# Holding back the loads of later batches, and new lengths for transfers in a planned kernel

## The chip, the cores and the metric

One core of one Trainium2 chip. The metric is the device time of one execution in microseconds (us). A kernel's figure is the median of its runs. A profiled execution has one span of its own, which is not the median. "Fast" and "slow" are the two states of a run; only fast runs enter the ratios.

## The reference

Attention whose keys and values are first projected from 1024 rows to 64, then an MLP over the tokens with a residual, then an MLP over the channels with a residual. Eight batches, eight heads, head size 64.

```python
def _attn_ref(q, k, v, E, F):
    k_proj = np.einsum('ks,bhsd->bhkd', E, k)
    v_proj = np.einsum('ks,bhsd->bhkd', F, v)
    ...  # softmax of q k_proj^T / 8
    return np.matmul(attn, v_proj)

def _moe_ref(x, w_tok1, w_tok2, w_ch1, w_ch2):
    xt = x.transpose(0, 2, 1)
    h = np.maximum(xt @ w_tok1, 0.0) @ w_tok2
    u = x + h.transpose(0, 2, 1)
    h2 = np.maximum(u @ w_ch1, 0.0) @ w_ch2
    return u + h2
```

## The kernel before

The kernel is software-pipelined over batches by a planner. Every piece of work is a job with an engine, an occupancy and a latency; the planner lays all jobs out in time by a simple model and the kernel then emits them in that order. The times of the model serve only to set the order. The kernel pins each engine's instructions to the order in which they are emitted, so on the chip an engine takes its jobs in that order and waits only for its data. The model knows one serial "DMA" engine, although loads go out from GpSimd's queue and transposes and stores from SyncE's. The page of the kernel before counts both queues against the same 16 DMA engines (q0, the loads, 43.2% of their time, and q1 29.4%), and a transpose of u beside loads lands late: 14.3 us after its issue at 137.82, behind five loads, against 4.2 at 90.0 behind one.

```python
    LAG = {"PE": 0.25, "DVE": 0.15, "ACT": 0.15, "POOL": 0.2, "DMA": 0.1}
    ...
    def sp(t, fn, **kw):                       # a transpose or a store, issued by SyncE
        return pl.add("DMA", t, t + 1.5, fn, **kw)

    def ld(mb, fn, **kw):                      # a load, issued by GpSimd
        t = mb / 0.40
        return pl.add("DMA", t, t + 2.0, fn, **kw)
    ...
    def q_transpose(due):
        for h in range(0, H, H // 2):
            sp(
                5.0,                           # planned length of a transpose of q
                lambda h=h: nc.sync.dma_start_transpose(out=qT[...], in_=q_sb[...]),
    ...
            sp(
                4.0,                           # planned length of a transpose of u
                lambda: nc.sync.dma_start_transpose(out=uT_t[i]..., in_=u_t[b % 2]...),
```

Per batch there are six loads (k, k, v, v, q, q: four heads each), two transposes of q into qT and two transposes of u into uT (each 128 x 2048 elements of 2 bytes, 512 KB). Right behind each uT come four sums and differences of quarters of uT on VectorE, the "S sums", which the channel MLP multiplies. VectorE's later work, such as the x_sb that TensorE needs for the next batch, stands behind the S sums in its order, so a late uT stops VectorE and then TensorE: in the trace before, VectorE waited 6.69 us for uT (until 152.17) and TensorE 6.46 us for x_sb (until 153.44).

The loads of batch b + 2 are made as jobs at the end of batch b's part:

```python
        if b + 2 < B:
            for name in "kvq":
                for hh in range(0, H, H // 2):
                    load_heads(b + 2, name, hh, H // 2, None)

    plan = pl.plan()
    for j in plan:
        j.fn()
        pin()
```

The softmax here doesn't subtract the row's maximum and nothing guards it: scores larger than these inputs give would overflow.

Of the kernel before, what the change touches and what calls it, by code (L numbers as in the profile page):

```python
# [12 lines left out]
ACT = mybir.ActivationFunctionType  # L13
# [21 lines left out]
class Planner:  # L35


    LAG = {"PE": 0.25, "DVE": 0.15, "ACT": 0.15, "POOL": 0.2, "DMA": 0.1}

    def __init__(self, caps, homes):  # L40
        self.jobs, self.caps, self.homes = [], caps, homes
# [30 lines left out]
    def plan(self):  # L72
# [15 lines left out]
        def open_(j):  # L88
            est[j.n] = max((d.end + self.LAG[d.eng] if d.eng != j.eng else d.full for d in j.deps), default=0.0)
            can.setdefault(j.eng, []).append(j)  # L90
# [83 lines left out]
def kernel(  # L174
# [13 lines left out]
    nc = tc.nc  # L188
# [27 lines left out]
    def pin():  # L216
        done = nc.cur_bb.bb.instructions
        for i in done[seen[0] :]:
            before = last.get(i.engine)
            if before is not None:  # L220
                tc.add_manual_dep(i, before, order, reason="program order")
            last[i.engine] = i.name
        seen[0] = len(done)
# [5 lines left out]
    def tile_of(shape, dtype, name):  # L229
        return sb.tile(shape, dtype, tag=name, name=name)  # L230
# [3 lines left out]
    def bank(b):  # L234

        return banks[b.at]
# [3 lines left out]
    o_t = [tile_of([P, 2, DM], F32, f"o{i}") for i in range(3)]  # L240
# [36 lines left out]
    for half in range(2):  # L277
# [3 lines left out]
    pl = Planner(  # L281
        {"U": 5, "D": 3, "F": 3, "S": 7},
        {"U": range(6), "D": range(6), "F": (5, 6, 7), "S": (0, 1, 2, 3, 4, 6, 7)},
    )
    MM = {512: 0.216, 256: 0.109, 130: 0.057, 128: 0.057, 64: 0.057}

    def pe(n, cols, fn, **kw):
        t = n * MM[cols]
        return pl.add("PE", t, t, fn, **kw)
# [11 lines left out]
        return pl.add("POOL", t, t, fn, **kw)  # L301

    def sp(t, fn, **kw):
        return pl.add("DMA", t, t + 1.5, fn, **kw)

    def ld(mb, fn, **kw):
        t = mb / 0.40
        return pl.add("DMA", t, t + 2.0, fn, **kw)


    def dma(dst, src):
        return lambda: nc.gpsimd.dma_start(out=dst, in_=src)

    def load_heads(b, name, h, hn, due):
        dst, src = {"k": (k_sb, k), "v": (v_sb, v), "q": (q_sb, q)}[name]
        hs = slice(h, h + hn)
        ld(
            0.262 * hn,
            dma(dst[:, hs], src[b, hs].rearrange("h (p si) d -> p h si d", p=P)),
            writes=[(name, i) for i in range(h, h + hn)], prio=due,  # L320
        )

    first = iter(range(-1000, 0))
    ld(1.0, dma(EF[0], E), writes=["E"], prio=next(first))
# [36 lines left out]
    def due_d(j, i):  # L361
        return TU * j + 23.8 + 1.76 * i
# [22 lines left out]
    for n, (src, dst) in enumerate(((EF[0], ET_sb), (EF[1], FT_sb))):  # L385
        b = Bank("F", full=False)
# [111 lines left out]
    def q_transpose(due):  # L498
        for h in range(0, H, H // 2):
            sp(  # L500
                5.0,
                lambda h=h: nc.sync.dma_start_transpose(
                    out=qT[:, h : h + H // 2].rearrange("p h j s -> p (h j) s"),
                    in_=q_sb[:, h : h + H // 2].rearrange("p h si d -> p (h si d)"),
                ),
                reads=[("q", i) for i in range(h, h + H // 2)],
                writes=[("qT", i) for i in range(h, h + H // 2)], prio=due,
            )
# [96 lines left out]
    def token2(b, si, due):  # L605
        bk = Bank(stream[0], full=False)

        def mm():
            for t in range(TC):
                nc.tensor.matmul(  # L610
                    bank(bk), wt2_sb[:, t, si::NSI], hT_sb[:, t, :],
                    start=(t == 0), stop=(t == TC - 1),
                )

        pe(
            TC, 512, mm, reads=["wt2"] + [("hT", t, hp) for t in range(TC) for hp in range(HP)],
            takes=[bk], prio=due,
        )
        dve(
            512,  # L620
            lambda: nc.vector.tensor_add(  # L621
                out=u_t[b % 2][:, si, :], in0=bank(bk), in1=x_sb[:, si, :]
            ),
            reads=[("x", h, si // NJ) for h in range(H)], writes=[("u", b % 2, si)], uses=[bk],
        )
        if si % NJ == NJ - 1:
            i = si // NJ
            sp(
                4.0,
                lambda: nc.sync.dma_start_transpose(  # L630
                    out=uT_t[i].rearrange("p s dc q -> p (s dc) q"),
                    in_=u_t[b % 2][:, i * NJ : (i + 1) * NJ].rearrange("p s d -> p (s d)"),
                ),
                reads=[("u", b % 2, n) for n in range(i * NJ, (i + 1) * NJ)],
                writes=[("uT", i, n) for n in range(HP)], prio=None,
            )
# [210 lines left out]
    out_v = out.rearrange("b (p si) d -> b p si d", p=P)  # L847

    def down_block(j):
        b, i = j // 2, j % 2  # L850
        G = G_t[j % 2]
        bk = {n: Bank("D", seeded=n == "y") for n in "xyz"}
        os = [(2 * j + sh) % 3 for sh in range(2)]

        def view(n):
            return bank(bk[n]).rearrange("p (t d) -> p t d", t=2)

        def u_of(sh, dh):
            rows = slice(i * NJ + 2 * sh, i * NJ + 2 * sh + 2)
            return u_t[b % 2][:, rows, dh * DH : (dh + 1) * DH]  # L860

        def u_key(sh):
            rows = range(i * NJ + 2 * sh, i * NJ + 2 * sh + 2)
            return [("u", b % 2, r) for r in rows] + ([("up", hp, i) for hp in range(HP)] if b == 0 else [])

        def o_of(sh, dh):
            return o_t[os[sh]][:, :, dh * DH : (dh + 1) * DH]

        def o_key(sh, dh):
            return ("o", os[sh], dh)  # L870

        def mm(n, t):
            for cc in range(C2):
                nc.tensor.matmul(  # L874
                    view(X_OF[n])[:, t, :], G[:, G_OF[n], cc, t * P : (t + 1) * P], w2_of(n, cc),
                    start=(n in (1, 7) and t == 0 and cc == 0), stop=(cc == C2 - 1),
                    skip_group_check=True,
                )

        def product(n, i):  # L880
            if n in (1, 2, 3):
                w = [("w2", {1: 0, 2: 1, 3: 1}[n], c) for c in range(2)]
            else:
                w = [("W2", c, n) for c in range(2)]
            bb = bk[X_OF[n]]
            for t in range(2):
                first = n in (1, 7) and t == 0
                pe(
                    C2, 256, lambda t=t: mm(n, t),
                    reads=w + [("G", j % 2, G_OF[n], m) for m in range(SETS)],  # L890
                    takes=[bb] if first else [], uses=[] if first else [bb],
                    prio=due_d(j, 2 * i + t),
                )

        def store(sh):
            rows = slice(i * NJ + 2 * sh, i * NJ + 2 * sh + 2)
            sp(
                2.0, lambda: nc.sync.dma_start(out=out_v[b, :, rows, :], in_=o_t[os[sh]]),
                reads=[o_key(sh, 0), o_key(sh, 1)], prio=None,
            )  # L900

        def copy_add(dst, key, src, sh, dh):
            act(512, lambda: nc.scalar.copy(out=dst, in_=view(src)), writes=[key], uses=[bk[src]])  # L903
            pool(
                512, lambda: nc.gpsimd.tensor_add(out=dst, in0=dst, in1=u_of(sh, dh)),  # L905
                reads=u_key(sh), writes=[key],
            )

        product(1, 0)
        act(  # L910
            512, lambda: nc.scalar.copy(out=view("y"), in_=view("x")), takes=[bk["y"]],
            uses=[bk["x"]],
        )
        product(7, 1)
        product(6, 2)
        copy_add(db, "db", "y", 1, 0)
        product(2, 3)
        copy_add(o_of(0, 0), o_key(0, 0), "x", 0, 0)
        product(5, 4)
        dve(  # L920
            512, lambda: nc.vector.tensor_add(out=da, in0=view("y"), in1=u_of(1, 1)),  # L921
            reads=u_key(1), writes=["da"], uses=[bk["y"]],
        )
        dve(
            512, lambda: nc.vector.tensor_add(out=o_of(1, 1), in0=view("z"), in1=da),  # L925
            reads=["da"], writes=[o_key(1, 1)], uses=[bk["z"]],
        )
        product(3, 5)
        copy_add(o_of(0, 1), o_key(0, 1), "y", 0, 1)
        store(0)  # L930
        product(4, 6)
        dve(
            512, lambda: nc.vector.tensor_add(out=o_of(1, 0), in0=view("z"), in1=db),
            reads=["db"], writes=[o_key(1, 0)], uses=[bk["z"]],
        )
        store(1)


# [51 lines left out]
    for b in range(B):  # L990
# [10 lines left out]
        if b + 2 < B:  # L1001
            for name in "kvq":
                for hh in range(0, H, H // 2):
                    load_heads(b + 2, name, hh, H // 2, None)

    plan = pl.plan()
    for j in plan:
        j.fn()
        pin()


# [28 lines left out]
```

## Time and profile before

| | before |
|---|---|
| median of 4 runs | 450.68 us (448.52 to 452.01) |
| profiled span | 452.1 us, mean TensorE clock 0.974 |

The prediction below shows the page, the windows with TensorE's four holes, and the chain. What it does not show is where the loads of batch 3 stand near the two uT transposes of batch 1, which were issued at 90.0 and 93.4 us. The timeline of GpSimd of the kernel before; columns are start and length of the issue, engine, line, operation, tiles, count, and in brackets what it waited for:

```profile
86.50 0.78 POOL L312 DMA_DIRECT2D k_sb<-in_k_dram  x1 [5.40 <-PE ps L445]
...
95.38 0.78 POOL L312 DMA_DIRECT2D k_sb<-in_k_dram  x1
96.15 1.50 POOL L312 DMA_DIRECT2D v_sb<-in_v_dram  x2
97.63 1.51 POOL L312 DMA_DIRECT2D q_sb<-in_q_dram  x2
```

One k load goes out 3.5 us ahead of the first transpose, and the other five behind the second. The view of the uT tile for 80 to 125 us gives landing times of 4.2 to 4.3 us, and nobody waits for them.

### The profile page before, as it was taken

The numbers are of one execution on the slowest core, as the hardware profiler recorded it, in microseconds if no ns is written. First come the engines' busy times: TensorE is split into PE (matmuls) and PEld (weight loads), VectorE is DVE, ScalarE is ACT, GpSimd is POOL, SyncE is SP. The second block draws the span as 40 slices with busy tenths as digits, with TensorE's granted clock in tenths as the row PEclk, the third lists the DMA queues.
The fourth block names the chain that finished last, engine by engine and source line by source line (L and its number), as shares of the span: only waits on it lengthen the run. The fifth ranks groups of instructions, "written<-read, shape, count | busy, mean of one in ns | idle before, by whom it ended". The sixth has DMA issues, their size and how long they took to land.

```text
span 452.1 us, 9325 instructions
## 1 busy us (share of the span) xinstructions
PE 420.0 (93%) x3736; PEld 338.3 (75%) x3736; DVE 324.0 (72%) x791; ACT 235.2 (52%) x431; POOL 106.5 (24%) x122
## 2 busy tenths in 40 slices
PE   4789999999999499997999999997999999999993
PEld 2578878677878378786787878786787877888883
DVE  2479989589887366977676885887677885875451
ACT  1347674367466154575447744575446654465530
POOL 7443041240041120412114021411102021213212
PEclk8599999999999799999999999999999999999998
DMA  8999989899959927899756996299150502240122
GB/s 118 207 202 205 207 131 175 167 186 206 186 82 196 197 41 160 150 168 188 141 127 105 203 160 141 51 183 228 54 94 1 141 1 95 48 139 39 57 95 93
DMA packets 89515, 60.63 MB, mean 134 GB/s; under 512 B 55680, under 2 KB 84864, under 8 KB 89472
## 3 DMA queue, kind: packets, MB, share of 16 engines
q0 software_dynamic: 30784, 29.63, 43.2%
q1 hardware_dynamic: 58688, 30.41, 29.4%
q8 instruction: 29, 0.48, 0.4%
q14 instruction: 14, 0.11, 0.1%
HBM read 59.24 MB, written 16.78 MB: 168 GB/s over the span
## 4 chain that ended last, share of the span: by engine, by line
PE 71%; DVE 13%; DMA 12%; issue 2%; ACT 1%; POOL 1%; DVEq 0%; ACTq 0%; POOLq 0%
PE ps L874 26%; PE ps L779 25%; DMA uT<-u 10%; PE ps L590 5%; PE ps L610 5%; PE ps L442 3%; DVE G L814 2%; PE ps L536 2%; PE ps L559 2%; DVE S L649 2%; DMA q_sb<-in_q_dram 2%; DVE x_sb L576 1%; DVE wT L403 1%; DVE u L706 1%; PE ps L520 1%
## 5 line engine op out<-in xcount | busy, mean ns | idle before, releaser
L874 PEld LDWEIGHTS <-G 128*128 128x128 bf16 x1344 | 130.6, 98 | 26.9 <-issue 3.8
L874 PE MATMUL ps<-wc_sb,G 128*128 128x256 bf16 x768 | 104.9, 274 | 1.9 <-DVE da L921 0.9
L801 ACT ACTIVATE G<-ps 128x512 bf16<-128x512 f32 x96 | 57.3, 599 | 57.4 <-PE ps L779 57.1
L779 PEld LDWEIGHTS <-wc_sb 128*128 128x128 bf16 x768 | 73.3, 98 | 15.4 <-issue 2.2
L874 PE MATMUL ps<-wT,G 128*128 128x256 bf16 x576 | 78.1, 273 | 1.0 <-DVE o L925 1.0
L905 POOL TENSOR_TENSOR o<-o,u 128x512 f32<-128x512 f32 x32 | 36.9, 1153 | 128.4 <-ACT o L903 128.4
L779 PEld LDWEIGHTS <-wT 128*128 128x128 bf16 x576 | 55.5, 98 | 15.3 <-issue 4.1
L905 POOL TENSOR_TENSOR db<-db,u 128x512 f32<-128x512 f32 x16 | 19.0, 1190 | 172.4 <-ACT db L903 172.4
L779 PE MATMUL ps<-S,wc_sb 128*128 128x256 bf16 x384 | 58.0, 274 | 0.0
L779 PE MATMUL ps<-uT,wc_sb 128*128 128x256 bf16 x384 | 57.5, 273 | 0.0
L779 PE MATMUL ps<-S,wT 128*128 128x256 bf16 x384 | 56.3, 276 | 0.2 <-DVE S L649 0.2
L576 DVE TENSOR_TENSOR x_sb<-ps,rdn 128x256 bf16<-128x256 f32 x128 | 50.7, 415 | 0.5
L760 DVE CUSTOM_DVE_ANT_0 g<-ps,ub 128x512 bf16<-128x512 f32 x48 | 32.7, 681 | 24.9 <-PE ps L779 24.9
L814 DVE TENSOR_TENSOR G<-G 128x512 bf16<-128x512 bf16 x96 | 44.6, 466 | 3.1
L621 DVE TENSOR_TENSOR u<-ps,x_sb 128x512 bf16<-128x512 f32 x56 | 37.9, 685 | 10.6 <-PE ps L610 10.3
L760 DVE CUSTOM_DVE_ANT_0 G<-ps,ua 128x512 bf16<-128x512 f32 x48 | 32.9, 685 | 16.2 <-ACT ua L807 15.4
L545 ACT ACTIVATE a<-ps 128x512 bf16<-128x512 f32 x64 | 37.5, 604 | 13.0 <-PE ps L536 12.8
L807 ACT COPY ua<-ps 128x512 f32<-128x512 f32 x48 | 28.2, 588 | 27.1 <-PE ps L779 26.6
L559 PE MATMUL ps<-vb,a 128*128 128x130 bf16 x256 | 32.0, 228 | 9.6 <-DVE x_sb L576 9.2
L807 ACT COPY ub<-ps 128x512 f32<-128x512 f32 x48 | 28.1, 586 | 21.3 <-PE ps L779 20.4
L559 PEld LDWEIGHTS <-a 128*128 128x128 bf16 x256 | 23.1, 102 | 13.6 <-issue 10.8
L610 PE MATMUL ps<-hT_sb,wt_sb 128*128 128x512 bf16 x112 | 32.6, 379 | 0.0
(71 smaller groups left out, 525.4 us busy)
## 6 DMA issues: line engine op xcount, KB each, us to landing
out_dram<-o SPq DMA_DIRECT2D x32, 512.0 KB, 3.5
k_sb<-in_k_dram POOLq DMA_DIRECT2D x14, 512.0 KB, 7.4
v_sb<-in_v_dram POOLq DMA_DIRECT2D x14, 512.0 KB, 9.4
q_sb<-in_q_dram POOLq DMA_DIRECT2D x14, 512.0 KB, 8.5
wc_sb<-in_moe_w_ch_dram POOLq DMA_DIRECT2D x6, 256.0 KB, 12.0
wc_sb<-in_moe_w_ch_dram POOLq DMA_DIRECT2D x4, 384.0 KB, 12.1
k_sb<-in_k_dram POOLq DMA_DIRECT2D x4, 256.0 KB, 9.1
v_sb<-in_v_dram POOLq DMA_DIRECT2D x4, 256.0 KB, 9.6
```

The costliest lines, as they stand in the source:

```text
L545: lambda: nc.scalar.activation(out=a_t[h % 4], in_=bank(bk), func=ACT.Exp, scale=scale),
L559: nc.tensor.matmul(view()[:, 2 * jj : 2 * jj + 2].rearrange("p c d -> p (c d)"), a_t[h % 4][:, j * P : (j + 1) * P], vb[:, h].rearrange("k ...
L576: lambda: nc.vector.tensor_tensor(out=x_sb[:, 4 * half : 4 * half + 4, h * D : (h + 1) * D], in0=view()[:, :, 0:D], in1=rdn[:, :, None].to ...
L610: nc.tensor.matmul(bank(bk), wt2_sb[:, t, si::NSI], hT_sb[:, t, :], start=(t == 0), stop=(t == TC - 1),)
L621: lambda: nc.vector.tensor_add(out=u_t[b % 2][:, si, :], in0=bank(bk), in1=x_sb[:, si, :]),
L760: nc.vector._custom_dve(TENSOR_ADD_SAT, out=out, in0=in0, in1=in1, s0=FMAX, s1=0.0)
L779: nc.tensor.matmul(t[:, c, :], w1_of(n, dd, 2 * m + c), a_of(j, n, dd), start=(n in (1, 7) and c == 0 and dd == 0), stop=(c == 1 and dd == 1),
L801: lambda: nc.scalar.activation(out=G[:, n, cs], in_=view(src), func=ACT.Relu),
L807: 512, lambda: nc.scalar.copy(out=dst, in_=view("y")), writes=[(name, s % 2)],
L814: 512, lambda: f(out=G[:, n, cs], in0=in0, in1=in1), ps=False, reads=deps,
L874: nc.tensor.matmul(view(X_OF[n])[:, t, :], G[:, G_OF[n], cc, t * P : (t + 1) * P], w2_of(n, cc), start=(n in (1, 7) and t == 0 and cc == 0 ...
L905: 512, lambda: nc.gpsimd.tensor_add(out=dst, in0=dst, in1=u_of(sh, dh)),
```

## The change

Its intent: loads of later batches should not pile up in the DMA engines ahead of the transfers that are wanted sooner. Each such load gets a semaphore wait (a "gate") on the last TensorE job that ends at least 1.5 us before the load in the plan. And the plan gets new numbers: what uses a transfer is planned 1.0 us after its end instead of 0.1, transposes and stores are planned shorter.

```diff
-    LAG = {"PE": 0.25, "DVE": 0.15, "ACT": 0.15, "POOL": 0.2, "DMA": 0.1}
+    LAG = {"PE": 0.25, "DVE": 0.15, "ACT": 0.15, "POOL": 0.2, "DMA": 1.0}
...
-        return pl.add("DMA", t, t + 1.5, fn, **kw)
+        return pl.add("DMA", t, t + 1.0, fn, **kw)
...  load_heads
+        if b > 1:
+            paced.add(j)
...  q_transpose
-                5.0,
+                3.5,
...  transpose of u
-                4.0,
+                3.5,
...  store
-                2.0, lambda: nc.sync.dma_start(...)
+                1.5, lambda: nc.sync.dma_start(...)
...  emitting the plan
+        if j.eng == "PE":
+            end_of[j] = new[-1].name
+        if j in paced:
+            done = [p for p in on_pe if p.end < j.start - 1.5]
+            tc.add_manual_dep(new[-1], end_of[done[-1]], gate, reason="pace of the loads")
```

More of the change, by code (lines that the diff above doesn't have):

```diff
@@ L312, in dma @@
         return lambda: nc.gpsimd.dma_start(out=dst, in_=src)
+    paced = set()
     def load_heads(b, name, h, hn, due):
@@ L316, in load_heads @@
         hs = slice(h, h + hn)
-        ld(
+        j = ld(
             0.262 * hn,
@@ L897, in store @@
             sp(
-                2.0, lambda: nc.sync.dma_start(out=out_v[b, :, rows, :], in_=o_t[os[sh]]),
+                1.5, lambda: nc.sync.dma_start(out=out_v[b, :, rows, :], in_=o_t[os[sh]]),
                 reads=[o_key(sh, 0), o_key(sh, 1)], prio=None,
@@ L1006 @@
     plan = pl.plan()
+    gate = mybir.DependencyInfo(mybir.DependencyClass.Sync, mybir.DependencyReason.DATA)
+    on_pe = [j for j in plan if j.eng == "PE"]
+    end_of = {}
     for j in plan:
+        n = len(nc.cur_bb.bb.instructions)
         j.fn()
+        new = nc.cur_bb.bb.instructions[n:]
+        if j.eng == "PE":
[3 more added lines that the diff above has]
+            tc.add_manual_dep(new[-1], end_of[done[-1]], gate, reason="pace of the loads")
         pin()
```

## The prediction

> **What bounds the kernel now.** I read the page first: TensorE is busy 93% of the span and its row of slices is full but for the start, the end and one dent, so the kernel is TensorE work plus holes in it.
>
> ```profile
> PE 420.0 (93%) x3736; PEld 338.3 (75%) x3736; DVE 324.0 (72%) x791; ACT 235.2 (52%) x431; POOL 106.5 (24%) x122
> ...
> PE   4789999999999499997999999997999999999993
> ...
> PEclk8599999999999799999999999999999999999998
> DMA  8999989899959927899756996299150502240122
> ```
>
> The reader is to see three things: the 4 and the 7 of TensorE in slices 14 and 19 (slices of 11.3 us), the 7 of the clock just after the first, and the DMA digits of 9 and 6 there. Next the windows, to size the holes (PE busy is the first number after the length).
>
> ```profile
> 97.00:145.00 48.00, 47.94 (x420) 38.15 (x419) 41.11 (x106) 30.62 (x57) 9.35 (x11) 1.00 0.95 169
> 145.00:153.00 8.00, 1.99 (x20) 1.56 (x18) 1.31 (x5) 2.36 (x5) 1.89 (x2) 0.96 1.30 184
> 153.00:163.00 10.00, 9.56 (x69) 7.64 (x69) 7.47 (x28) 3.42 (x6) 0.81 (x1) 0.69 0.81 154
> ...
> 195.00:209.00 14.00, 11.42 (x108) 9.62 (x107) 8.82 (x26) 8.36 (x16) 2.90 (x3) 1.00 1.17 188
> 247.00:262.00 15.00, 14.50 (x140) 12.38 (x138) 11.87 (x37) 10.41 (x20) 3.05 (x3) 1.00 1.25 191
> 298.00:313.00 15.00, 12.83 (x122) 10.90 (x120) 10.21 (x31) 9.19 (x18) 2.71 (x3) 1.00 1.23 193
> ```
>
> Idle TensorE: 6.0, 2.6, 0.5 and 2.2 us; and after the first hole the granted clock is 0.69 for 10 us. Then the chain in order of time, for what ends those holes, and the timeline around the first one.
>
> ```profile
> 137.82 14.33 DMA uT<-u
> ...
> 196.82 10.30 DMA uT<-u
> ...
> 248.56 9.68 DMA uT<-u
> ...
> 299.05 11.51 DMA uT<-u
> ```
>
> ```profile
> 128.82 1.53 POOL L312 DMA_DIRECT2D k_sb<-in_k_dram  x2 [3.72 <-PE ps L445]
> ...
> 132.92 0.79 POOL L312 DMA_DIRECT2D v_sb<-in_v_dram  x1
> ...
> 135.68 0.78 POOL L312 DMA_DIRECT2D v_sb<-in_v_dram  x1
> ...
> 136.46 0.75 POOL L312 DMA_DIRECT2D q_sb<-in_q_dram  x1
> ...
> 137.82 9.65 SPq L630 DMA_TRANSPOSE uT<-u  x1
> ...
> 152.17 0.43 DVE L649 TENSOR_TENSOR S<-uT 128x512 bf16<-128x512 bf16 x1 [6.69 <-DMA uT<-u]
> ...
> 153.44 0.37 PE L559 MATMUL ps<-vb,a 128*128 128x130 bf16 x2 [6.46 <-DVE x_sb L576]
> ```
>
> ```profile
> DVE S L649 <- DMA uT<-u: 12.2, 4, 6.7
> DMA to landing us min/median/max: 4.2/4.5/14.3
> ```
>
> The transpose of u into uT lands in 4.2 to 4.5 us when little else is moving (median of 14). The second one of a batch is issued just behind a burst of loads of the batch after next, and then takes 9.7 to 14.3 us. VectorE stands in program order at the S sums that read uT, so its later x_sb work, and then TensorE, stop with it. This happens four times, 12.2 us on VectorE, 6.46 + 2.58 + 0.50 + 2.23 = 11.8 us on TensorE (the timeline's waits for x_sb).
>
> A small model fits all four: stall = landing time less the work ordered between the transpose's release and the S sums. By the timeline VectorE reached the sums at 152.17 - 6.69 = 145.48, 7.7 us after the issue: 14.3 - 7.7 = 6.6. The others: 10.3 - 8.0, 9.7 - 9.0, 11.5 - 9.0, that is 2.3, 0.7, 2.5.
>
> [...] a transpose from SP goes from 4.2 to 14.3 us beside loads from GpSimd. [...] 6.46 us idle, then clock 0.69 over 10 us, while the holes under 2.6 us left it at 1.00.
>
> **The change part by part.** Nothing is computed less or more: 3736 matmuls, 68 loads, 26 transposes, 32 stores as before. Compared by engine order:
>
> (a) The numbers of the plan. Transposes are planned shorter and their users a little later, loads' users 0.9 us later. TensorE's order is the same up to some 92 us of plan, differs in small swaps from there to about 154 and again from 185 to 206, and is then the same but for one swap. So startup (TensorE busy 29.5 of the first 40 us) and tail are untouched, worth 0.
>
> (b) q loads move. Those of batches 3, 4 and 5 come much earlier in the GpSimd queue: before, a batch's q followed its k and v; now it precedes them. Of batch 4 both q loads leave the burst ahead of the 137.82 transpose (one of them was issued there at 136.46).
>
> (c) The gates, 36 of them. I count TensorE work in program order, at 0.109 us per 256-column and 0.216 us per 512-column matmul (eight L779 take 0.87 us, four L590 0.86 us in the chain), between a gate's matmul and the one that releases the transpose. Batch 4, first stall: gates at -10.7, -7.6, -5.4 and +2.6 us. Traced before: issues at -9.0, -8.2, -4.9, -2.1, and q at -1.4. So the fourth load moves from ahead of the transpose to after it, and q is gone. A lone load lands about 5.6 us after issue and a queued one follows each 2.2 to 2.6 us, so the third load lands about when the transpose starts. I put the transpose at 5.5 to 7 us. The S sums stand 6.35 us of TensorE work behind the release (7.8 before; here the plan gives less room). Stall 0 to 0.7 instead of 6.6, and no half clock.
>
> Second stall (batch 5): gates at -10.7, -7.6, -5.0, -2.6. The first still waits for the projection that frees k_sb (-8.3), and an add precedes the fourth in the queue, at -0.4, as before (issued -0.9). Sums at 8.3, before 8.2. The only help is that q, issued at 184.19, no longer delays k and v. I take off 0.6 of 2.6.
>
> Third and fourth stall: gates at -10.0, -7.0, -4.4, -2.0, and the loads stand at -7.6, -5.0, -2.2, 0.0 in the order, as before; sums at 9.6 both before and after. The gates are already open when the queue gets there, or hold the third load by 2 us, which joins a queue that is still draining. Worth 0.
>
> (d) Clock. At 0.5 for 6.8 us of the 10-us window, 10 x 0.31 = 3.1 us of full-clock work; some of it would have been idle, so 2.6.
>
> Sum on the traced run: -6.5 (first hole) - 2.6 (clock) + 0.4 (rest of the first stall) - 0.6 = -9.3. The traced run is a slow one (453.87 us against a median of 450.19, lowest 448.52), and part of those 3.7 us may be a longer first stall or its half clock. I take 85 to 90% of it for the median: -8.2, so 442.0 us.
>
> **Rivals.** (R1) The loads' bursts matter everywhere and spacing them mends all four stalls. For it: all four have the same shape. Against: at stalls two to four the gates don't reach past the transpose. It would give another 5 us: 437.
> (R2) A new stall. The loads of batch 3's q now sit at -7.6 and -5.0, k at -2.2 before the first transpose of batch 1 (issued 90.02), with 6.0 us of work to its first use; and the first transpose of batch 2 has 6.3 us of room instead of 9.8. Against: with one load 3.5 us ahead the former took 4.24 us, and the latter's loads are gated to -5.2 and +2.4. It would cost 1 to 4 us: 443 to 446.
> (R3) Gates hold the GpSimd queue, so adds, stores and VectorE's use of db come late. [...] Against: GpSimd is busy 24% and its adds wait for ACT anyway; the gates name matmuls planned over 1.5 us earlier. It would cost 0 to 2 us, and lateness here makes the program slower than 450 only if it hits VectorE's sums in every batch.
> (R4) The first stall goes but the freed time is lost at the next transpose. Against: the stalls are counted from each release, not from absolute time. It would leave 446 to 449.
>
> **Range and chances.** 2% faster is 441.2 us, within 1 us of the sum, so the verdict is near a coin's toss: faster 0.42, within 2% 0.55, slower 0.03. The range 437 to 447 spans R1 at one end and R2 with half the gain at the other.
>
> **What would show each step.** Right: the dent in TensorE's slices and the clock's 7 near 150 us gone; longest wait of the S sums for uT down from 6.7 to under 3; that transpose 5.5 to 7 us; two or three uT transposes of 9 to 11 us still on the chain, near 190, 240 and 290 us; wait total 12.2 down to about 5. Wrong: all late transposes down to 5 us (R1), a wait for uT or qT before 130 us (R2), VectorE waiting for GpSimd's adds (R3).

## The result, and the profile after

| | before | after |
|---|---|---|
| median of 4 runs | 450.68 us (448.52 to 452.01) | 463.45 us (459.95 to 463.98) |
| profiled span | 452.1 us, clock 0.974 | 462.0 us, clock 0.969 |

The ratio is 1.0272, with a 95% interval of 1.0206 to 1.0338: slower. A ratio is the mean time of one kernel's fast runs over that of the other's in the same rounds, so it is not quite the ratio of the medians.

The page of the changed kernel, in 40 slices of 11.55 us: TensorE, its clock, the DMA engines, and what they moved.

```profile
PE   5699999917899999998999999998999999999993
...
PEclk9799999977799999999899999999999999999999
DMA  8999999999998997299733997289241502240122
GB/s 128 207 200 206 196 171 162 184 97 86 129 195 134 219 188 172 47 136 229 119 111 61 177 229 174 47 138 227 51 103 33 138 1 93 45 138 28 66 93 92
```

The old dent of TensorE near 150 us is gone. A deeper one, the 1 and the 7, stands at 92 to 116 us, with three slices at clock 0.7. In the same slices the DMA row shows 9 and the engines move 97 and 86 GB/s, about half of the 162 to 207 of the seven slices ahead of them. Busy engines that move little: that is where to look.

The windows of the changed kernel (stretch, length, then TensorE's busy time first; clock, DMA share and GB/s last):

```profile
94.00:105.00 11.00, 1.29 (x11) 0.94 (x9) 0.74 (x3) 0.98 (x3) 0.78 (x1) 0.73 1.30 96
105.00:112.00 7.00, 7.00 (x49) 5.26 (x48) 3.13 (x12) 4.32 (x9) 0.88 (x2) 0.70 1.43 101
112.00:118.00 6.00, 0.70 (x8) 0.50 (x6) 1.62 (x6) 1.48 (x4) 0.61 (x1) 0.84 1.33 63
118.00:145.00 27.00, 27.00 (x204) 20.37 (x203) 22.77 (x59) 13.32 (x24) 2.76 (x4) 0.91 1.20 182
```

```profile
163.00:170.00 7.00, 6.53 (x63) 5.43 (x61) 6.93 (x22) 4.54 (x9) 2.30 (x2) 1.00 1.21 202
```

TensorE idles 9.7 us and 5.3 us in the two new holes. The last line is where the same work now stands behind which the kernel before idled 6.0 us: the S sums of batch 2's second half, some 17 us later in the trace. There 0.5 us of idle is left. What ended the new holes, from TensorE's timeline and the list of waits:

```profile
104.28 1.01 PE L783 MATMUL ps<-uT,wc_sb 128*128 128x256 bf16 x4 [9.71 <-DMA uT<-u]
...
117.74 0.38 PE L563 MATMUL ps<-vb,a 128*128 128x130 bf16 x2 [5.30 <-DVE x_sb L580]
```

```profile
DVE S L653 <- DMA uT<-u: 21.9, 5, 12.0
```

TensorE waited for the first uT itself, and then for x_sb, which stood on VectorE behind the second uT. VectorE's waits for uT went from 12.2 us to 21.9. The uT view for 85 to 100 us and the chain give the transposes:

```profile
DMA to landing us min/median/max: 16.4/19.8/23.2
```

```profile
93.15 23.21 DMA uT<-u
...
155.71 6.84 DMA uT<-u
206.07 9.63 DMA uT<-u
259.17 9.10 DMA uT<-u
309.08 10.54 DMA uT<-u
```

The two transposes of batch 1, which took 4.2 and 4.3 us before, take 16.4 (issued at 87.81) and 23.2 us (93.15). The loads of batch 3 around them, from GpSimd's timeline:

```profile
82.30 0.78 POOL L312 DMA_DIRECT2D q_sb<-in_q_dram  x1 [3.38 <-PE ps L594]
84.09 0.74 POOL L312 DMA_DIRECT2D q_sb<-in_q_dram  x1 [1.01 <-PE ps L449]
...
87.82 0.79 POOL L312 DMA_DIRECT2D k_sb<-in_k_dram  x1 [0.20 <-issue]
...
94.90 0.78 POOL L312 DMA_DIRECT2D k_sb<-in_k_dram  x1 [1.65 <-PE ps L563]
108.80 0.74 POOL L312 DMA_DIRECT2D v_sb<-in_v_dram  x1 [13.12 <-PE ps L783]
```

The order is now q q k | uT uT | k v v, where it was k | uT uT | k v v q q. Two q loads stand ahead of the first transpose within 5.5 us and a k goes out in the same moment (87.82 against 87.81), where one k load stood 3.5 us ahead before; the next k goes out beside the second. ("Three loads ahead" below means these three.)

The books of the two traces: TensorE's idle time in the stretches named (9.7, 5.3 and 0.5 us above, and 2.1 and 1.6 us at 213 to 223 and 313 to 323 us) is 19.2 us; before it was 11.3 (the four holes in the prediction): +7.9. The clock costs, estimated as length times what is missing to 1.00, 7 x 0.30 + 27 x 0.09 = 4.5 us in the windows at 105 and 118, and up to 10 x 0.17 = 1.7 at 213 (clock 0.83); before 3.1: +1.4 to +3.1. Together +9.3 to +11.0, against a difference of the spans of 9.9.

### The profile page after: what moved, and what is told of

Its sections match the earlier page's. It is cut to its first block, busy times and chain, and to the rows that moved or that the text cites. A ratio compares the mean times of both kernels' runs of the same rounds, so it can differ in the third digit from the quotient of the medians.

```text
span 462.0 us, 9343 instructions
## 1 busy us (share of the span) xinstructions
PE 422.6 (91%) x3736; PEld 339.0 (73%) x3736; DVE 324.3 (70%) x791; ACT 235.6 (51%) x431; POOL 106.7 (23%) x122
## 4 chain that ended last, share of the span: by engine, by line
PE 66%; DMA 14%; DVE 14%; issue 2%; ACT 1%; POOL 1%; DVEq 0%; ACTq 0%; POOLq 0%
PE ps L878 25%; PE ps L783 23%; DMA uT<-u 13%; PE ps L594 5%; PE ps L614 5%; DVE G L818 3%; DVE S L653 3%; PE ps L446 2%; PE ps L563 2%; PE ps L540 2%; DVE x_sb L580 2%; DMA q_sb<-in_q_dram 1%; DVE wT L407 1%; DVE u L710 1%; DVE g L764 1%
## 5 line engine op out<-in xcount | busy, mean ns | idle before, releaser
L783 PEld LDWEIGHTS <-wc_sb 128*128 128x128 bf16 x768 | 74.5, 100 | 25.7 <-issue 12.2
L783 PE MATMUL ps<-uT,wc_sb 128*128 128x256 bf16 x384 | 59.7, 280 | 9.7 <-DMA uT<-u 9.7
L783 PEld LDWEIGHTS <-wT 128*128 128x128 bf16 x576 | 56.2, 99 | 13.1 <-issue 1.1
L783 PE MATMUL ps<-S,wc_sb 128*128 128x256 bf16 x384 | 58.6, 276 | 0.0
L783 PE MATMUL ps<-S,wT 128*128 128x256 bf16 x384 | 56.7, 277 | 0.2 <-DVE S L653 0.2
L818 DVE TENSOR_TENSOR G<-G 128x512 bf16<-128x512 bf16 x96 | 45.6, 478 | 3.2
L764 DVE CUSTOM_DVE_ANT_0 G<-ps,ua 128x512 bf16<-128x512 f32 x48 | 32.9, 686 | 18.4 <-ACT ua L811 17.9
L824 ACT COPY ps<-ps 128x512 f32<-128x512 f32 x48 | 27.8, 578 | 22.4 <-PE ps L783 19.7
L563 PEld LDWEIGHTS <-a 128*128 128x128 bf16 x256 | 23.1, 102 | 15.3 <-issue 12.2
```

The costliest lines, as they stand in the source:

```text
L563: nc.tensor.matmul(view()[:, 2 * jj : 2 * jj + 2].rearrange("p c d -> p (c d)"), a_t[h % 4][:, j * P : (j + 1) * P], vb[:, h].rearrange("k ...
L764: nc.vector._custom_dve(TENSOR_ADD_SAT, out=out, in0=in0, in1=in1, s0=FMAX, s1=0.0)
L783: nc.tensor.matmul(t[:, c, :], w1_of(n, dd, 2 * m + c), a_of(j, n, dd), start=(n in (1, 7) and c == 0 and dd == 0), stop=(c == 1 and dd == 1),
L818: 512, lambda: f(out=G[:, n, cs], in0=in0, in1=in1), ps=False, reads=deps,
L824: 512, lambda: nc.scalar.copy(out=view("y"), in_=view("x")), takes=[bk["y"]],
```

## The experiments

My theory, after the result: the planner's numbers and the gates are harmless by themselves; the place of the loads beside the uT transposes makes the loss. Rivals: the gates hold GpSimd's queue; the planner numbers cost something in every batch; or two kinds of transfer spoil each other's rate whenever they overlap, wherever they stand. "e1" to "e4" and "e7" to "e11" compute the reference correctly. "e5", "e6", "e8" and "e12" move data only and give zeros on purpose.

### e1 and e2: the two halves of the change

e1 is the kernel before with the gates; e2 is the changed kernel without them.

```diff
 e1 (against before)                       e2 (against after)
+        if b > 1:                         -        if j in paced:
+            paced.add(j)                  -            done = [...]
+ ... the gate of the change               -            tc.add_manual_dep(...)
```

> The gates alone, with the plan and the order of the kernel before. Theory A (overlap: loads and transposes in flight together make both several times slower, and the changed order of batch 3's loads puts two q loads and a k load beside the transposes of batch 1): the order is that of before, one k load is nearly landed when the transpose of batch 1 starts, so both transposes of batch 1 land in 4 to 6 us; the gates keep the last v load and the q loads away from the transpose at 138 us, whose 14.3 us fall to 6 to 9 us: 441 to 446 us. Theory B (the gates themselves do the harm, by holding the GpSimd queue and the loads): 456 us or more.

> The changed plan and order, without the gates. Theory A: the q loads of batch 3 still go ahead of its k, so the transposes of batch 1 near 88 and 93 us take over 10 us each and TensorE stands there for 8 us or more: 456 to 468 us. Theory B: without the gates the loss is gone: 440 to 451 us.

Measured: e1 444.28 us (442.62 to 448.3), ratio 0.9875 (0.9808 to 0.9941). e2 464.55 us (461.06 to 467.92), ratio 1.0285 (1.0213 to 1.0358), within the interval of the changed kernel. The gates alone gain 1.2%, which is under the 2% mark but clear of noise; the plan alone loses all of what the change loses. So it is not the gates. In e1 the transpose that took 14.3 us in the kernel before takes 8.3, by the chain of e1:

```profile
135.93 8.28 DMA uT<-u
```

The wait for it is 0.6 us instead of 6.7. The other three stay (9.8, 9.9 and 10.5 us in the same chain), as the prediction had said of the gates. In e1 the two transposes of batch 1 took 5.7 and 4.3 us, as expected. In e2 the first took 13.8 and the second 23.73 us, as in the changed kernel, though no gate held the v loads, which went out at 95.2 us:

```profile
92.59 23.73 DMA uT<-u
```

### e3 and e4: other places for batch 3's loads in the changed kernel

e3 puts batch 3's loads back in the order of the kernel before. e4 leaves q ahead and holds k and v until both transposes have landed.

```diff
 e3                                        e4
+        if b == 3:                        +        if b == 3 and name in "kv":
+            if name == "q":               +            j.deps.update(turns[1])
+                j.deps.update(kv3)        +            held.add(j)
+            else:                         ...
+                if kv3:                   +        if j in held:
+                    j.deps.update(turns[1])  +         tc.add_manual_dep(new[-1],
+                kv3.append(j)             +                end_of[turns[1][1]], gate, ...)
```

> The changed kernel with one thing undone: batch 3's loads in the order of before (one k load, the two transposes of batch 1, then k, v, v, q, q); gates and plan numbers stay, and batches 4 to 7 keep the changed order. Theory A: both transposes of batch 1 land in 4 to 7 us, the 9.9 and 5.5 us holes of TensorE near 94 and 112 us are gone, and the hole of 6.6 us that before had at 147 us stays gone: 440 to 446 us. Theory B: the gates are all there, so 456 us or more.

> The changed kernel with one dependence added: the k and v loads of batch 3 wait for both transposes of batch 1 to land; its q loads stay first, gates and plan numbers stay. If the loss near 94 and 112 us comes from the k loads that run beside those transposes while q loads are still queued, both transposes of batch 1 land in 4 to 8 us, no hole over 3 us there, and the time is 440 to 452 us. If it comes from the q loads alone, or from the gates, the first transpose still takes over 12 us and the time stays at 457 us or more.

Measured: e3 450.67 us, ratio 1.0022 (0.9963 to 1.0081). The two transposes took 4.4 and 4.3 us and both holes were gone: moving the loads of one batch gives back the whole loss. The view of the two:

```profile
DMA to landing us min/median/max: 4.3/4.4/4.4
```

But I had expected 440 to 446, and missed that: the move pushed a stall to the next place. Batch 2's second uT took 11.0 us, and VectorE waited:

```profile
147.50 0.42 DVE L662 TENSOR_TENSOR S<-uT 128x512 bf16<-128x512 bf16 x1 [4.86 <-DMA uT<-u]
```

Its room, by the count of the prediction, is 6.35 us in the new plan and was 7.8 in the old, and 11.0 - 6.35 = 4.65.

Measured: e4 451.9 us, fast runs 448.46 to 453.62, ratio 1.0041 (0.9958 to 1.0125). Its profile fell in the slow state (459.02 us), so its landing times are those of a slow run, and no fast run shows them: the two transposes took 7.4 and 4.3 us. The k and v loads, now issued one every 2 to 3 us from 99.5 us on, met the qT transposes instead, issued at 100.3 and 108.2, which took 20.7 and 17.1 us, and the uT at 121.5 took 17.8. In that run the collision had moved: the loads were spaced by gates and yet met in the worst way.

### e5 and e6: loads and transposes with nothing else running

e5 starts six loads (1 MB of float32 read, 512 KB written as bf16 each), six transposes, and mixtures of them. e6 starts six loads, and transposes join when the first load has landed.

```python
    for i in range(N):                       # e5, block 4
        load(i, 2)
        turn(i)
    ...
    for i in range(N):                       # e6, block 1
        load(i, 0)
    landed(0)                                # the first load is there
    join(0)                                  # now one transpose
```

> A kernel of transfers alone (its output is zeros on purpose), in six phases: six loads of 4 heads; six transposes of 128x2048; six loads and one transpose; six loads and six transposes; two of each; six loads and six stores. If the work only adds up on the 16 engines (a load 2.5 us, a transpose 2.3 us of them, plus 2 to 3 us at the end): 18, 17, 20, 32, 12 and 25 us. Theory A: the phases with both kinds are far over the sum, six and six over 50 us, two and two over 16 us, while loads with stores stay near the sum.

> Transfers alone again, zeros as output. The phases before let the transposes start ahead of the loads and the work simply added up (six and six: 33.9 us of 18.4 and 16.8). Here the transposes join when the first of six loads has landed. If joining late is what makes the mixture slow (theory A in a narrower form), six loads and two transposes take over 30 us, and six and six over 45 us. If transfers among themselves always add up, the four phases take some 21, 23, 34 and 26 us, and the slow mixture of the whole kernel needs a further cause in it.

Measured in e5: six loads 18.4 us (one lands every 2.5 us), six transposes 16.8 (the first lands after 4.4, then one every 2.4 us), six and six 33.9. The work of the two kinds adds up, and the theory that they spoil each other's rate whenever they overlap falls in this plain form. Measured in e6: six loads and one transpose 21.6 us in all, six and six 33.5, so again nothing is lost. But the single transpose, which carries 2.4 us of work by the interval in e5, landed late. Its landing time (issued at 23.24), and the packets of the loads (q0) and of the transpose (q1) from 28 to 36 us:

```profile
DMA to landing us min/median/max: 15.7/15.7/15.7
```

```profile
q0 software_dynamic: 1242, 1.24, 91.3%
q1 hardware_dynamic: 1238, 0.32, 31.0%
```

This reading is one key to the size. The columns are packets, megabytes written and share of time. Both queues got the same number of packets, but a load's packet carries four times the bytes. At these sizes the 512 KB of a transpose make 2048 packets of 256 bytes, and those of a load 512 of 1 KB (in e12's stretch of six and six every 6.5 us the queues had 12480 and 3168 packets, 2080 and 528 for each transfer). As an estimate from these counts: if the two kinds go on one for one, as from 28 to 36 us, a transpose that joins a long row of loads lands only when about 2048 load packets, four loads, have gone by. All six loads were issued before this transpose. Loads issued after one can delay it too: in e5 the first transpose of the six and six, issued 0.3 us ahead of the first of six loads, took 9.3 us.

The hole of the changed kernel does not go by this count. Its packets from 94 to 105 us:

```profile
q1 hardware_dynamic: 2147, 0.54, 96.5%
q0 software_dynamic: 518, 0.51, 33.1%
```

Four transpose packets went by for one load packet, though a k load was under way all the time (issued at 87.82 and 94.90, landed after 14.2 and 20.3 us). And a transpose packet took longer. Worked out from share x length x 16 engines / packets, it took 79 ns here, 32 ns in e6 above, and 22 ns in the six transposes alone of e5 (12480 packets, 94.1% of 18 us). So by these counts the transposes were not queueing behind many load packets in this stretch; the engines spent longer on each of their own. e2 has the same stretch without gates: 2073 to 571 packets and 99 GB/s from 94 to 105 us.

### e7: a rule for the order, on the old plan

e1, with v loads from batch 3 on held until the second uT transpose of the batch two before has landed.

```diff
+        if b > 2 and name == "v":
+            j.deps.add(turns[b - 2][1])
+            held[j] = turns[b - 2][1]
...
+        if j in held:
+            tc.add_manual_dep(new[-1], end_of[held[j]], gate, reason="after the transpose")
```

> The gates alone on the plan of before, and the v loads of each batch held until the second transpose of the batch two before has landed, so that only two k loads, not four loads, are ahead of it. The late transposes, 8.3 to 10.5 us with the gates alone, should land in 4.3 to 6.5 us, inside the 8 to 9 us of work ordered before their users, and the last three stalls (some 5 us of TensorE in all) go: 437 to 441 us. If the v loads were not what slows them, the time stays at 444 us.

Measured: 438.63 us (437.03 to 439.3), ratio 0.9762 (0.970 to 0.9824), the best of all kernels here. It is faster than the kernel before; whether by 2% stays unclear, as the interval crosses 0.98. VectorE's waits for uT:

```profile
DVE S L658 <- DMA uT<-u: 1.9, 4, 0.9
```

They were 12.2 us before and 6.2 in e1. The four late transposes took 8.5, 6.6, 5.1 and 7.0 us; I had expected 4.3 to 6.5, so three of them were later than that, and the time came out because they nearly fit the room (0.9 us was the longest wait). At the first, a q load had gone out 4.7 us ahead as well (131.12 against 135.85), so it stood behind two k loads and a q.

### e8: the changed kernel's issue times with nothing else running

> Zeros on purpose; transfers alone, in four blocks. Block A issues six loads, four transposes and a store at the times after the first load at which the changed kernel issued them (transposes at 5.5, 10.9, 23.7 and 41.2 us), with nothing else running. If the slow mixture comes of how the transfers meet, the first two transposes take 14 to 18 and 18 to 25 us as in the changed kernel (16.4 and 23.2). If it needs what the rest of the kernel does at the time, they take about 10 to 14 us each. Block B repeats six loads and two transposes that join late (23.7 us when first measured). Block C is B with three and five packets of 2 KB, which go to some of the engines only, ahead of the transposes: if a transpose's packets on all 16 engines wait for the slowest engine, C takes over 27 us; if not, under 25. Block D is six loads and six late transposes with three single packets: 33 to 35 us if nothing waits, over 38 if it does.

Block A issues each transfer at a tick of a chain of ScalarE copies, block C adds three and five packets of 2 KB, fewer than the 16 engines, ahead of the transposes.

```python
    for t, what, i in plan:                  # block A, e.g. (5.5, "t", 0)
        ...
        tc.add_manual_dep(ins(), ticks[round(t / TICK)], gate, reason="clock")
```

Measured: in block A the first transpose took 12.0 us and the second about 13 (from its issue to its last packet); one load issued beside the second took 12.8 instead of 5.6. That is the rival's 10 to 14, not the 14 to 25 of the kernel, so the issue times of this stretch alone do not make the whole delay. What the rest of the kernel adds (transfers still under way at 82 us, the work of the other engines) was not tested. Still, from 35 to 43 us the engines in block A moved 102 GB/s with packets under way nearly all the time. Blocks B and C took the same time, 23.6 and 23.7 us, and block D 33 us, no more than the sum. So my idea that a few uneven packets make a transpose's 16 engines wait for each other found no support.

### e9 and e10: which number moved the loads

By the plan, it is the length of q transposes that moves q ahead of k in the order. e9 is the kernel before with that one number, no gates. e10 is the changed kernel with that one number back.

```diff
 e9 (against before)       e10 (against after)
-                5.0,      -                3.5,
+                3.5,      +                5.0,
```

> The kernel before with one number of the change: the q transposes planned 3.5 us long instead of 5.0, no gates. The plan then puts one q load of batch 3 ahead of batch 1's two uT transposes, so two loads (q, k) stand ahead of the first instead of one. If loads ahead are what makes those transposes late, the first takes 8 to 12 us instead of 4.2 against some 6 us of room, a hole of 2 to 5 us appears near 94 us on top of the four old stalls, and the time is 450 to 458. If the loads' places have no part in it, 448 to 451 and no hole there.

> The changed kernel with that one number back at 5.0 us, all else as changed, gates too. No q load of batch 3 stands ahead of batch 1's transposes, but k and v do: two loads instead of three, and two instead of three still to come. My theory: the first transpose takes 8 to 12 us, the holes near 94 and 112 us shrink from 15.3 us together to 2 to 6, and the time is 445 to 455. If q's place were not the cause, 460 to 465 as the changed kernel.

Measured, in the same rounds: e9 451.57 us, ratio 0.9988 (0.9915 to 1.0061); e10 448.93 us, ratio 0.9949 (0.989 to 1.0008). The transposes of batch 1 in e10:

```profile
DMA to landing us min/median/max: 5.4/6.6/7.8
```

The time of e10 is as expected: with two k loads ahead of the first transpose (3.5 and 0.3 us) it took 7.8 us, just under the 8 to 12 written, and TensorE waited for uT only 0.9 us, not 2 to 6. That single number undoes all of the loss. e9 missed: q and k stand ahead of the first transpose, but 6.4 and 3.5 us ahead, and the transpose took 5.1 us, where I had expected 8 to 12. So the number alone is harmless as well, and the loss comes only of both together. Only then do both q loads and a k go out ahead of or with the transpose, within 5.5 us (6.4 in e2), with a k right behind it. Four cells: 451.2 us before, 451.6 with this number, 448.9 with all the rest, and 463.5 (of other rounds) with both. Effects of an order do not add.

### e11: the rule on the changed kernel

The changed kernel, all numbers and gates kept; from batch 3 on q follows k and v, and v is held as in e7.

```diff
+            if name == "v":
+                j.deps.add(turns[b - 2][1])
+                held[j] = turns[b - 2][1]
+            if name == "q":
+                j.deps.update(kv[b])
```

> The changed kernel with all its numbers and gates, but from batch 3 on q loads follow k and v, and v loads wait for the second uT transpose of the batch two before. Two k loads stand ahead of batch 1's transposes. If where loads stand is all that is wrong with the changed kernel, 437 to 444 and no wait for uT over 3 us. If its planned numbers cost something of themselves, 446 or more with holes elsewhere.

Measured: 441.03 us (439.4 to 443.72), ratio 0.9791 (0.9739 to 0.9843), as expected; faster than before, and by 2% or not is again unclear. Later transposes took 4.2 to 6.0 us; one hole of 3 us is left at 94 us, where two k loads stand ahead and the transpose takes 9.5. With where the loads stand mended, the changed kernel's numbers and gates are some 5% better than with its own order.

### e12: one, two and three loads ahead, and a steady stream

> Zeros on purpose; transfers alone, by a clock of ScalarE work. Alone a load takes 5.6 us and a transpose 4.4. Four blocks of one load and one transpose issued 0, 1.2, 2.4 and 3.6 us after it, two with the load 1.2 and 2.4 us after the transpose, then two and three loads ahead of one transpose, then six and six issued alternately every 3 us and every 6 us. If work in the engines simply adds up, packet by packet, the transpose of a pair lands 4.5 to 7 us after its issue, behind two loads in 7 to 9, behind three in 10 to 12; six and six every 3 us take about 34 us as they did in one burst, and every 6 us some 38, each transpose in 5 to 7. If a load and a transpose that meet out of step slow each other over their sum, as the landing of 12.8 us for one load beside one transpose in the last run suggests, the transposes of pairs take over 8 us at some distances, six and six every 3 us take over 40 us, and every 6 us each transpose takes 9 us or more.

```python
    block([(0.0, "l", 0), (1.8, "l", 1), (3.6, "l", 2), (3.6, "t", 0)])
    block([x for i in range(6) for x in ((3.0 * i, "l", i), (3.0 * i + 1.8, "t", i))])
    block([x for i in range(6) for x in ((6.0 * i, "l", i), (6.0 * i + 1.8, "t", i))])
```

The landing times of the transposes, first behind three loads, then in the middle of the stream with a pair every 3.2 us (the two issued from 104 to 112 us), then with a pair every 6.5 us:

```profile
DMA to landing us min/median/max: 12.0/12.0/12.0
```

```profile
DMA to landing us min/median/max: 5.8/12.0/18.2
```

```profile
DMA to landing us min/median/max: 6.3/6.4/6.7
```

A transpose issued with a load took 7.9 us, 1.0, 2.3 and 3.6 us after it 6.9, 5.5 and 4.3, with the load 1.6 or 2.9 us behind it 4.3, behind two loads 9.0, behind three 12.0. These are near what adding up packet by packet gives, except for the 7.9 (7 was the most I had written). In the fast stream the first transpose took 5.8 us, the next ones 18.2, 20.5 and 10.1, loads some 16; all six and six took 39.8 us where one burst took 33.5, between the 34 and the "over 40" of the two theories. So in a stream each transfer lands late, and some rate is lost too. The rate, in 40 slices of 112 to 137 us of that stream:

```profile
GB/s 151 170 175 196 99 76 84 106 124 90 98 101 107 105 108 147 175 178 188 197 196 195 192 195 193 199 194 195 197 203 161 148 138 128 128 134 120 62 63 121
```

With the DMA row at 9 throughout, it goes between some 195 GB/s, as in the bursts, and 60 to 110. The changed kernel's 96, 101 and 63 GB/s are the lower of these. What puts the engines into the slower way of going is open: in these runs it shows only where transposes and loads arrive in turns (102 GB/s from 35 to 43 us in e8), not in bursts (195 GB/s from 28 to 36 us in e6), and three uneven packets did not bring it about in e8. A transpose packet takes longer in it (79 ns in the changed kernel's hole against 32 in e6, above).

## Why the prediction was wrong

The prediction said 442.0 us and a range of 437 to 447; the kernel took 463.45.

**What held.** Part (c) for the first stall: batch 2's second transpose, issued at 155.71, took 6.8 us (5.5 to 7 was written), and TensorE waited 0.5 us (0 to 0.7 was written); e1 shows that gates alone do much of it. The stalls two to four: transposes of 9.6, 9.1 and 10.5 us are still on the chain, as written. The sign of that gain was right and its size too high: e1 gains 1.25%, some 5.6 us, against the 8.2 of the sum. The clock fell after the long hole as it had in the kernel before (6.46 us idle, then 0.69 over 10 us): 9.71 us idle, then 0.70 over 7 us. But "the holes under 2.6 us left it at 1.00" is no rule: in the changed kernel two holes of 1.1 and 1.0 us, at 215.5 and 217.0 us, were followed by a clock of 0.50 from 219 to 221 us. A gate does hold GpSimd: in the changed kernel it stood for 13.12 us before it issued the v load of 108.8 us, and the trace names L783 on TensorE, which does not use v_sb, as what ended the wait.

**Which step failed.** Part (b), "q loads move", priced the move only where it helps: q leaves the burst ahead of 137.82. Its cost was put off to rival (R2), which named the very place, batch 3's q at the first transpose of batch 1 with 6.0 us of room, and gave it 1 to 4 us, "with one load 3.5 us ahead the former took 4.24 us". The step is that term, and it was wrong in two ways. First, it took the delay of one load for that of three: alone, e12 shows 4.3 us with one load 3.6 us ahead, 9.0 behind two and 12.0 behind three, and the prediction's own trace had 14.33 us behind five. (On the chip the k went out with the transpose, not 2.2 us ahead as counted.) Second, it took the work of the engines as fixed, a queued load each 2.2 to 2.6 us. In the changed kernel they fell to 96, 101 and 63 GB/s, and a transpose packet took 79 ns instead of 32. The second transpose, with the first one ahead of it in its queue and a k load issued 1.8 us after it, took 23.2 us. With 16.4 us put in, the prediction's own model gives the hole: 16.4 - 6.0 = 10.4, measured 9.7. The model of room was right and its input was not.

How much each weighs can be estimated. With the 12.0 us of e12 (and of e8) the first transpose lands at 99.8, and TensorE, which ran dry at 94.6, stands for some 5.3 us. With the 13 us of e8 the second lands at 106.2; VectorE reached its S sums 6.3 us after TensorE went on, which would then be at 106.2 too, so the second hole closes. So, as an estimate, transfers at these times make about 5 of the 15.0 us of idle when nothing else runs, and some 10 come only in the whole kernel, where the engines go slower for longer. No run separates the two inside the kernel.

A smaller slip in part (b): "before, a batch's q followed its k and v" holds for batches 3 and 4. Batch 5's q loads already went ahead (169.34 and 184.19, its k at 187.97).

What comes after the first hole is a chain: a clock of 0.50 until 109 us (0.70 over 105 to 112 us), the gates that released v at 108.8 only after the stall so that the v loads met a qT transpose (issued at 105.97, landed after 20.6 us), a second hole of 5.3 us. The gates are not needed for it, as e2 loses as much without them. R2's 1 to 4 us became 15.0 us of idle and some 4.5 us of lost clock, and it took back the gain.

**The other rivals.** R1, all stalls mended by spacing, is refuted for the gates but right as an idea: e7 and e11 all but mend them by order (longest waits of VectorE for uT 0.9 and 2.1 us) and come out at 438.6 and 441.0. R3, gates that hold GpSimd, is refuted as the cause of the loss by e1 and e2. R4 has a share of truth in e3: there a mended stall came back at the next transpose.

**What stays open.** That the place of batch 3's loads makes the loss is shown by e2, e3 and e10. Why the engines go slower in that stretch is open. Of the first transpose's 16.4 us the three loads explain 12.0 and of the second's 23.2 us e8 gives 13; the rest the runs show but don't explain.

## What to carry to other kernels

Where a queue of loads and a queue of wanted transfers meet, look for how many loads go out within five or six us ahead of each wanted transfer and beside it (here three within 5.5 us went with a transpose of 16.4 us, and two, 6.4 and 3.5 us ahead, with one of 5.1 in e9), not for whether each load is held; a hold that frees a load into a transposing stretch only moves the collision (the v loads of 108.8 and 111.9 us met a qT transpose, which took 20.6 us). Any change to a planner's numbers is a change to an order: list what moved ahead of every transfer that has a deadline, and price each with its size in packets and its room. And a rival that names the right place deserves a size from the worst case in the old trace (14.33 us here), not from the mildest (4.24).
